# Feed-forward weights in runs of rows per partition, equal column groups, a block transposition on VectorE and a result kept by column groups

## The chip, the cores and the metric

The kernel runs on one core of a Trainium2 chip. The metric is the device time of one execution in microseconds; the median of three runs of the kernel before is 1333.5. Engines are named as the profile names them: PE is TensorE's matmul stream and PEld its weight loads, DVE is VectorE, ACT is ScalarE, POOL is GpSimd, SP is SyncE, which issues the large loads. All data are 32-bit floats.

## The reference, cut to what matters

One decoder block for one new token of each of two sequences (B = 2, D = 512, 32 heads of 128, 8192 cached positions, F = 1792):

```python
def _A_ref(x, k_cache, v_cache, wq, wo):
    q = (x @ wq).reshape(B, Sq, H, Dh).transpose(0, 2, 1, 3)
    scores = jnp.einsum("bhqd,bhkd->bhqk", q, k_cache) * (Dh ** -0.5)
    p = _softmax(scores, axis=-1)
    o = jnp.einsum("bhqk,bhkd->bhqd", p, v_cache)
    return o.transpose(0, 2, 1, 3).reshape(B, Sq, H * Dh) @ wo

def _B_ref(x, w_gate, w_up, w_down):
    return (_silu(x @ w_gate) * (x @ w_up)) @ w_down

h = x + _A_ref(_layernorm(x), k_cache, v_cache, wq, wo)
h2 = h + _B_ref(_layernorm(h), w_gate, w_up, w_down)
```

K and V together are 537 MB, the feed-forward weights 11 MB.

## The kernel before

**The stream.** Everything large goes through one ring of five slots of 4 MB, in the order in which it is used. `order` lists the transfers, `load` issues one on SP's queue, `pump` issues as many as slots are free, and `used` frees a slot. A K or V of one head of one sequence is one transfer, that of the last two pairs four pieces. The three feed-forward weights come last: `w_gate` and `w_up` in four pieces each (128 rows of the matrix, one on each partition, 7 KB a row), `w_down` in pieces of four, four, four, one and one blocks of 128 rows (2 KB a row). A DMA on SP also waits for the DMA eight before it, whose semaphore it takes over.

**Attention.** For pair i (a head and a sequence) VectorE multiplies K by q (L209) and sums (L212), the maximum goes over the partitions through PE (L224, L228, L230), ScalarE takes the exponential (L235), and PE multiplies P by V one pair later (`pv`, L250): 64 blocks of 128 x 128 with one-column weights, block j into column group j % 4 of the array, so that four matmuls run side by side. `project_o` (L273) adds the heads' part of the output into `attn`.

**The tail.** After the last pair come the residual `h1` (L330), the second norm (`layernorm`, L155 to L166) with four transpositions into `hT` (two of 32 columns used, the others zero), and then:

- `project_f` (L340), gate, then up: F is cut in 14 blocks of 128 columns that go round the four column groups, so two groups have four blocks (512 columns) and two have three (384). Each group's result lies on 32 partitions of the PSUM tile `psf`; two memsets (L305) fill what no matmul writes.
- `sg` is the gate times its sigmoid (L352, L353), `gu` the product with up (L356).
- Four transpositions on PE (L359) turn `gu`, and VectorE copies them to `gT` (L361).
- The down projection: 12 of the 14 blocks go round the column groups into `y_ps` (L371). VectorE and ScalarE copy it out in halves as `ysb` (L379, L380), and a matmul with `pick` (L385), a matrix of ones and zeros made at L310, sums the four groups into `f_ps`, which holds the residual already (L366) and to which the last two blocks add directly (L386).
- `res` is copied from `f_ps`, 2 x 512 (L390), and stored by SP (L391).

The schedule is manual: on every engine instructions run in the order of the code. A 32-bit matmul is two instructions of PE in the profile, each with a weight load.

Of the kernel before, what the change touches and what calls it, by code (L numbers as in the profile page):

```python
# [19 lines left out]
def tile_decode_block(  # L20
# [36 lines left out]
    # Everything large streams through one ring of equal slots, in the order of its use. A whole  # L57
    # K or V of one head is one transfer, but for the first and the last ones.
# [22 lines left out]
    order += [(("wg", 0), c, 1) for c in range(DC)] + [(("wu", 0), c, 1) for c in range(DC)]  # L81
    order += [(("wd", 0), c, n) for c, n in ((0, 4), (4, 4), (8, 4), (12, 1), (13, 1))]
# [5 lines left out]
    def load(item, e, n):  # L88
# [16 lines left out]
        elif kind == "wo":  # L105
            nc.sync.dma_start(
                t[:, : G * D].rearrange("p (c m) -> p c m", c=G),
                wo[i * G * DH : (i + 1) * G * DH, :].rearrange("(c p) m -> p c m", p=P),
            )
        elif kind in ("wg", "wu"):  # L110
            src = w_gate if kind == "wg" else w_up
            nc.sync.dma_start(t[:, e * F : (e + 1) * F], src[e * P : (e + 1) * P, :])
        else:
            nc.sync.dma_start(
                t[:, e * D : (e + n) * D].rearrange("p (c m) -> p c m", c=n),
                w_down[e * P : (e + n) * P, :].rearrange("(c p) m -> p c m", p=P),
            )
# [52 lines left out]
    xT_ps = layernorm(xs, "x")  # L170
# [129 lines left out]
    # Blocks of 128 columns go round the four column groups of the tensor engine.  # L300
    TAIL = FB % 4
    psf = []
    for n in range(2):
        t = psum.tile([P, 4, P], F32, name="wide", bufs=2)
        nc.vector.memset(t[64:, TAIL + 1 :, :], 0.0)  # L305
        psf.append(t)

    pick = const.tile([P, B], F32, name="pick")
    for b in range(B):
        nc.vector.tensor_reduce(  # L310
            pick[:, b : b + 1],
            ident.rearrange("p (t r) -> p r t", t=4)[:, b, :],
            axis=AX.X,
            op=OP.add,
        )

# [14 lines left out]
    hT_ps = layernorm(h1, "h")  # L331
    nc.vector.tensor_copy(hT[:, :, :B], hT_ps)

    def project_f(kind, ps):
        wt = slot[(kind, 0)]
        for c in range(DC):
            w = wt[:, c * F : (c + 1) * F].rearrange("p (k m) -> p k m", m=P)
            for t in range(4):
                nb = len(range(t, FB, 4))
                nc.tensor.matmul(  # L340
                    ps[32 * t : 32 * t + 32, :nb, :],
                    hT[:, c, :],
                    w[:, t::4, :],
# [20 lines left out]
    w = slot[("wd", 0)][:, : FB * D].rearrange("p (k m) -> p k m", k=FB)  # L364
    f_ps = psum.tile([B, D], F32, name="small", bufs=3)
    nc.tensor.matmul(f_ps, ident[:B, :B], h1, start=True, stop=False)  # L366
    y_ps = psum.tile([P, D], F32, name="wide", bufs=2)
    grouped = FB - TAIL
    for k in range(grouped):
        n, t = divmod(k, 4)  # L370
        nc.tensor.matmul(  # L371
            y_ps[32 * t : 32 * t + 32, :],
            gT[:, n, 32 * t : 32 * t + 32],
            w[:, k, :],
            start=(k < 4),
            stop=(k >= grouped - 4),
        )
    ysb = const.tile([P, D], F32, name="ysb")
    nc.vector.tensor_copy(ysb[:, : D // 2], y_ps[:, : D // 2])  # L379
    nc.scalar.activation(ysb[:, D // 2 :], y_ps[:, D // 2 :], AF.Copy)  # L380
    res = const.tile([B, D], F32, name="res")
    for k in range(grouped, FB):
        n, t = divmod(k, 4)
        if k == FB - 1:
            nc.tensor.matmul(f_ps, pick, ysb, start=False, stop=False)  # L385
        nc.tensor.matmul(  # L386
            f_ps, gT[:, n, 32 * t : 32 * t + B], w[:, k, :], start=False, stop=(k == FB - 1)
        )
    used(("wd", 0))
    nc.vector.tensor_copy(res, f_ps)  # L390
# [41 lines left out]
```

## Time and profile before

| | |
|---|---|
| three runs | 1332.21, 1333.50, 1333.54 us, median 1333.5 |
| the profiled execution, span of the core | 1329.8 us |
| DVE busy in the span | 1159.4 us (87%) |
| PE busy, weight loads | 585.3 us (44%), 374.0 us (28%) |
| ACT busy | 80.8 us (6%) |
| moved by DMA | 565.91 MB, mean 426 GB/s |

The span runs from the first to the last instruction of one profiled execution; the runs' times are those of whole executions and 2.4 to 3.7 us longer. Times in the rows are counted from the span's start. A timeline row gives the start, the length, the engine, the line, the operation, what it writes and reads, and in brackets how long the engine was idle before it and who ended that. [...] A DMA share is that of 16 DMA engines.

### The profile page before, as it was taken

Reading aid. Unit: us, or ns where it says so; the run is one execution under the profiler, and the core shown is the slowest. Engines: PE = TensorE matmul, PEld = TensorE weight load, DVE = VectorE, ACT = ScalarE, POOL = GpSimd, SP = SyncE. Lnnn points to the kernel's source line nnn. Section 1 sums busy time; section 2 is a strip of 40 time slices with the busy share of each in tenths; the row PEclk is TensorE's granted clock in tenths of the full one; section 3 lists DMA queues with packets and bytes.
Section 4 is the critical chain, followed back from the end, with each engine's and each line's share of the span. In section 5 each row is a group of like instructions: output and inputs, shape, how many; then the busy total and the mean of one; then the engine's idle time right before and its main releaser. Section 6 shows DMA issues by size and latency. Waiting matters only on the chain.

```text
span 1329.8 us, 19379 instructions
## 1 busy us (share of the span) xinstructions
PE 585.3 (44%) x9004; PEld 374.0 (28%) x9004; DVE 1159.4 (87%) x486; ACT 80.8 (6%) x341; POOL 1.9 (0%) x9
## 2 busy tenths in 40 slices
PE   5443433436633424433744334334375344344447
PEld 2322322223322322322412223222242222223322
DVE  6999999988899989997889989998879989999881
ACT  1000000000100000000100000000010000000001
POOL 0000000000000000000000000000000000000000
PEclk9656666667857566666886576666597666566668
DMA  9999999999999999999999999999999999999997
GB/s 398 437 432 433 430 433 430 435 429 428 432 432 432 433 430 434 431 429 435 427 430 436 428 438 427 436 428 429 431 414 433 431 433 431 434 430 433 422 401 279
DMA packets 30408, 565.91 MB, mean 426 GB/s; under 512 B 2676, under 2 KB 2676, under 8 KB 11640
## 3 DMA queue, kind: packets, MB, share of 16 engines
q1 hardware_dynamic: 30324, 564.67, 99.1%
q8 instruction: 70, 1.15, 0.3%
q14 instruction: 10, 0.08, 0.0%
q10 hardware_dynamic: 4, 0.00, 0.0%
HBM read 564.66 MB, written 0.00 MB: 425 GB/s over the span
## 4 chain that ended last, share of the span: by engine, by line
issue 98%; PE 1%; DVE 0%; DMA 0%; POOLq 0%; POOL 0%; ACT 0%
PE wide L340 1%; PE wide L371 0%; DMA xs<-in_A_x_dram 0%; PE small L385 0%; PE small L366 0%; PE small L386 0%; DVE gu L356 0%; DVE ln_stats L155 0%; DVE res L390 0%; PE small L359 0%; POOLq L427 0%; PE small L166 0%; DVE ln_y L163 0%; POOL ln_rstd L161 0%; DVE ysb L379 0%
## 5 line engine op out<-in xcount | busy, mean ns | idle before, releaser
L209 DVE TENSOR_TENSOR ring<-ring,qsb 128x4096 f32<-128x4096 f32 (+1 forms) x134 | 566.3, 4226 | 116.5 <-DMA ring<-in_A_k_cache_dram 105.5
L212 DVE TENSOR_REDUCE s<-ring 128x32 f32<-128x4096 f32 (+1 forms) x134 | 565.7, 4222 | 0.3
L250 PE MATMUL opart<-ring,p 128*1 128x128 f32 x8192 | 350.7, 351 | 165.2 <-DMA ring<-in_A_v_cache_dram 165.2
L250 PEld LDWEIGHTS opart<-ring,p 128*1 128x1 f32 x8192 | 247.1, 107 | 254.8 <-DMA ring<-in_A_v_cache_dram 170.2
L230 PE MATMUL small<-gm,nscale 1*128 1x1 f32 x128 | 35.8, 346 | 304.8 <-DVE gm L228 304.8
L224 PE MATMUL small<-ident,m 128*1 128x128 f32 x128 | 28.4, 310 | 210.3 <-DVE m L220 210.3
L230 PEld LDWEIGHTS small<-gm,nscale 1*128 1x128 f32 x128 | 30.3, 292 | 313.6 <-DVE gm L228 310.1
L224 PEld LDWEIGHTS small<-ident,m 128*1 128x1 f32 x128 | 5.5, 81 | 231.1 <-DVE m L220 228.8
L187 PE MATMUL wide<-ring,xb 128*128 128x512 f32 x128 | 58.7, 618 | 3.0 <-DMA ring<-in_A_wq_dram 3.0
L239 PE MATMUL small<-rs,ones 128*128 128x1 f32 x128 | 36.1, 351 | 46.9 <-ACT p L235 46.9
L263 ACT ACTIVATE osb<-opart 128x128 f32<-128x128 f32 x64 | 17.7, 277 | 530.6 <-PE opart L250 530.6
L239 PEld LDWEIGHTS small<-rs,ones 128*128 128x128 f32 x128 | 30.6, 297 | 52.4 <-ACT p L235 52.4
L273 PE MATMUL attn<-ring,oT 128*2 128x512 f32 x64 | 34.5, 698 | 0.3 <-ACT oT L266 0.3
L187 PEld LDWEIGHTS wide<-ring,xb 128*128 128x128 f32 x128 | 25.0, 198 | 34.1 <-issue 34.1
L232 ACT ACTIVATE nb<-small 128x1 f32<-128x1 f32 x64 | 10.9, 171 | 371.4 <-PE small L230 371.0
L265 PE MATMUL small<-r,osb 128*128 128x1 f32 x128 | 29.4, 299 | 2.0 <-ACT osb L263 2.0
L228 DVE TENSOR_REDUCE gm<-small 1x1 f32<-1x128 f32 x64 | 17.4, 272 | 14.7 <-PE small L224 14.7
L265 PEld LDWEIGHTS small<-r,osb 128*128 128x128 f32 x128 | 24.0, 235 | 20.6 <-issue 17.2
L266 ACT ACTIVATE oT<-small 128x1 f32<-128x1 f32 x64 | 11.0, 171 | 234.9 <-PE small L265 234.9
L235 ACT ACTIVATE p<-s,nb 128x64 f32<-128x64 f32 x64 | 22.3, 348 | 2.1
L243 DVE RECIPROCAL r<-small 128x1 f32<-128x1 f32 x64 | 10.1, 157 | 9.2 <-PE small L239 9.2
L220 DVE TENSOR_REDUCE m<-s 128x1 f32<-128x64 f32 x64 | 14.1, 220 | 2.2
(51 smaller groups left out, 66.1 us busy)
## 6 DMA issues: line engine op xcount, KB each, us to landing
ring<-in_A_k_cache_dram SPq DMA_DIRECT2D x61, 4096.0 KB, 39.8
ring<-in_A_v_cache_dram SPq DMA_DIRECT2D x61, 4096.0 KB, 30.8
ring<-in_A_k_cache_dram SPq DMA_DIRECT2D x12, 1024.0 KB, 19.6
ring<-in_A_v_cache_dram SPq DMA_DIRECT2D x12, 1024.0 KB, 19.8
ring<-in_A_wq_dram SPq DMA_DIRECT2D x4, 2048.0 KB, 35.2
ring<-in_A_wo_dram SPq DMA_DIRECT2D x4, 2048.0 KB, 17.2
ring<-in_B_w_gate_dram SPq DMA_DIRECT2D x4, 896.0 KB, 19.2
ring<-in_B_w_up_dram SPq DMA_DIRECT2D x4, 896.0 KB, 18.0
```

The source lines that it names most:

```text
L187: nc.tensor.matmul(ps, xb[:, c * B + b, :], w[:, c, n : n + 512], start=(c == 0), stop=(c == DC - 1),)
L209: nc.vector.tensor_tensor(kt, kt, qb, op=OP.mult)
L212: nc.vector.tensor_reduce(st[i]["s"][:, j0 : j0 + n], k_view(i, j0, n), axis=AX.X, op=OP.add)
L224: nc.tensor.matmul(st[i]["mrow"], st[i]["m"], ident, start=True, stop=True)
L228: nc.vector.tensor_reduce(gm, st[i]["mrow"], axis=AX.X, op=OP.max)
L230: nc.tensor.matmul(nb_ps, nscale, gm, start=True, stop=True)
L235: nc.scalar.activation(st[i]["p"], st[i]["s"], AF.Exp, bias=nb, scale=SCALE, accum_out=rs)
L239: nc.tensor.matmul(st[i]["den"], ones, rs, start=True, stop=True)
L250: nc.tensor.matmul(o[32 * t : 32 * t + 1, :], st[i]["p"][:, j : j + 1], vt[:, j, :], start=(j < 4), stop=(j >= NJ - 4),)
L263: nc.scalar.activation(osb, opart[i % 2], AF.Copy)
L265: nc.tensor.matmul(ot_ps, osb, st[i]["r"], start=True, stop=True)
L273: nc.tensor.matmul(attn, oT[:, h, :], w[:, h - g * G, :], start=(h == 0), stop=(h == H - 1))
```

## The change

- `order` and `load`: partition p of a slot now holds a run of neighbouring rows of the matrix, rows 4p to 4p+3 of `w_gate` and `w_up` and rows 14p to 14p+13 of `w_down`. `w_gate` is one transfer of 28 KB a partition, `w_up` two of 14 KB, `w_down` pieces of eight, four, one and one blocks (16, 8, 2 and 2 KB a partition).
- `layernorm` takes the columns for the second norm's transpositions in steps of four, to match.
- `project_f` gives each column group a quarter of F, 448 neighbouring columns. The memsets and `pick` are gone, and the two PSUM tiles are taken when they are used.
- `f_ps` becomes 128 x 128: column group t holds columns 128t to 128t+127 of the result on 32 partitions. Four matmuls put the residual there, ahead of the gate's.
- `gu` is written in the order (block, element), and one 32 x 32 block transposition on VectorE makes `gT` from it.
- The down projection adds all 14 blocks in all four column groups straight onto `f_ps`, 56 matmuls of 128 columns.
- `res` is 128 x 128; each sequence's row of the result leaves from four partitions, one by SP's queue and one by ScalarE's.

```diff
-    order += [(("wg", 0), c, 1) for c in range(DC)] + [(("wu", 0), c, 1) for c in range(DC)]
-    order += [(("wd", 0), c, n) for c, n in ((0, 4), (4, 4), (8, 4), (12, 1), (13, 1))]
+    order += [(("wg", 0), 0, DC)] + [(("wu", 0), c, 2) for c in range(0, DC, 2)]
+    order += [(("wd", 0), c, n) for c, n in ((0, 8), (8, 4), (12, 1), (13, 1))]
...
-            nc.sync.dma_start(t[:, e * F : (e + 1) * F], src[e * P : (e + 1) * P, :])
+            nc.sync.dma_start(
+                t[:, e * F : (e + n) * F],
+                src.rearrange("(p c) f -> p (c f)", p=P)[:, e * F : (e + n) * F],
+            )
         else:
             nc.sync.dma_start(
-                t[:, e * D : (e + n) * D].rearrange("p (c m) -> p c m", c=n),
-                w_down[e * P : (e + n) * P, :].rearrange("(c p) m -> p c m", p=P),
+                t[:, e * D : (e + n) * D],
+                w_down.rearrange("(p c) m -> p (c m)", p=P)[:, e * D : (e + n) * D],
             )
...
-            nc.tensor.transpose(yt[:, c, :], y[:, c * P : (c + 1) * P], ident[:B, :B])
+            cols = y.rearrange("b (p c) -> b c p", c=DC) if runs else y.rearrange("b (c p) -> b c p", c=DC)
+            nc.tensor.transpose(yt[:, c, :], cols[:, c, :], ident[:B, :B])
...
-    TAIL = FB % 4
-    psf = []
-    for n in range(2):
-        t = psum.tile([P, 4, P], F32, name="wide", bufs=2)
-        nc.vector.memset(t[64:, TAIL + 1 :, :], 0.0)
-        psf.append(t)
-
-    pick = const.tile([P, B], F32, name="pick")
-    for b in range(B):
-        nc.vector.tensor_reduce(
...
-    def project_f(kind, ps):
-        wt = slot[(kind, 0)]
+    f_ps = psum.tile([P, P], F32, name="small", bufs=3)
+    for t in range(4):
+        nc.tensor.matmul(
+            f_ps[32 * t : 32 * t + 32, :],
+            ident[:B, :32],
+            h1[:, t * P : (t + 1) * P],
+            start=True,
+            stop=False,
+        )
+
+    def project_f(kind):
+        ps = psum.tile([P, FQ], F32, name="wide", bufs=2)
         for c in range(DC):
-            w = wt[:, c * F : (c + 1) * F].rearrange("p (k m) -> p k m", m=P)
+            w = slot[(kind, 0)][:, c * F : (c + 1) * F]
             for t in range(4):
-                nb = len(range(t, FB, 4))
                 nc.tensor.matmul(
-                    ps[32 * t : 32 * t + 32, :nb, :],
+                    ps[32 * t : 32 * t + 32, :],
                     hT[:, c, :],
-                    w[:, t::4, :],
+                    w[:, t * FQ : (t + 1) * FQ],
...
-    gu = const.tile([P, 4 * P], F32, name="gu")
-    nc.vector.tensor_mul(gu, up, sg)
-    gT_ps = psum.tile([P, 4, P], F32, name="small", bufs=3)
-    for n in range(4):
-        nc.tensor.transpose(gT_ps[:, n, :], gu[:, n * P : (n + 1) * P], ident)
-    gT = const.tile([P, 4, P], F32, name="gT")
-    nc.vector.tensor_copy(gT, gT_ps)
...
+    gu = const.tile([P, FQ], F32, name="gu")
+    nc.vector.tensor_mul(
+        gu.rearrange("p (c j) -> p j c", c=FB),
+        up.rearrange("p (j c) -> p j c", c=FB),
+        sg.rearrange("p (j c) -> p j c", c=FB),
+    )
+    gT = const.tile([P, FQ], F32, name="gT")
+    nc.vector.transpose(gT, gu)
+
+    w = slot[("wd", 0)]
+    for c in range(FB):
+        for t in range(4):
+            nc.tensor.matmul(
+                f_ps[32 * t : 32 * t + 32, :],
+                gT[:, c * 32 : (c + 1) * 32],
+                w[:, c * D + t * P : c * D + (t + 1) * P],
+                start=False,
+                stop=(c == FB - 1),
+            )
     used(("wd", 0))
+    res = const.tile([P, P], F32, name="res")
     nc.vector.tensor_copy(res, f_ps)
-    nc.sync.dma_start(out.rearrange("b s d -> (b s) d"), res)
+    for b, queue in enumerate((nc.sync, nc.scalar)):
+        queue.dma_start(out[b, 0, :].rearrange("(t m) -> t m", t=4), res[b::32, :])
```

On SP's queue, the feed-forward weights at the end of the stream. Before (DMAHW names the semaphore of the transfer eight places earlier, DVE and PE the last user of the slot):

```order
L112 DMA ring<-in_B_w_gate_dram 128x1792 [waits DMAHW3_49,DVE_49]
L112 DMA ring<-in_B_w_gate_dram 128x1792 [waits DMAHW4_49]
L112 DMA ring<-in_B_w_gate_dram 128x1792 [waits DMAHW5_49]
L112 DMA ring<-in_B_w_gate_dram 128x1792 [waits DMAHW6_49]
L112 DMA ring<-in_B_w_up_dram 128x1792 [waits DMAHW7_49,DVE_49]
L112 DMA ring<-in_B_w_up_dram 128x1792 [waits DMAHW0_49]
L112 DMA ring<-in_B_w_up_dram 128x1792 [waits DMAHW1_49]
L112 DMA ring<-in_B_w_up_dram 128x1792 [waits DMAHW2_49]
L114 DMA ring<-in_B_w_down_dram 128x4x512 [waits DMAHW3_49,PE_49]
L114 DMA ring<-in_B_w_down_dram 128x4x512 [waits DMAHW4_49]
L114 DMA ring<-in_B_w_down_dram 128x4x512 [waits DMAHW5_49]
L114 DMA ring<-in_B_w_down_dram 128x512 [waits DMAHW6_49]
```

and now, with the store behind them:

```order
L112 DMA ring<-in_B_w_gate_dram 128x7168 [waits DMAHW3_49,DVE_49]
L112 DMA ring<-in_B_w_up_dram 128x3584 [waits DMAHW4_49,DVE_49]
L112 DMA ring<-in_B_w_up_dram 128x3584 [waits DMAHW5_49]
L117 DMA ring<-in_B_w_down_dram 128x4096 [waits DMAHW6_49,PE_49]
L117 DMA ring<-in_B_w_down_dram 128x2048 [waits DMAHW7_49]
L117 DMA ring<-in_B_w_down_dram 128x512 [waits DMAHW0_49]
L117 DMA ring<-in_B_w_down_dram 128x512 [waits DMAHW1_49]
L380 DMA out_dram<-res 4x128 [waits DMAHW3_49,DVE_49]
```

Thirteen transfers became seven. The first piece of `w_down` now waits for the transfer that held semaphore 6 (that of `wo`) instead of the first piece of `w_gate`.

On PE, from the last up matmuls on. Before:

```order
L359 MATMUL small<-ident,gu 128x128 [waits DVE_49]
L359 MATMUL small<-ident,gu 128x128 x3
L366 MATMUL small<-h_6392,ident 2x512
L371 MATMUL wide<-ring,gT 32x512 [waits DMAHW3_49,DVE_49]
L371 MATMUL wide<-ring,gT 32x512 x3
L371 MATMUL wide<-ring,gT 32x512 [waits DMAHW4_49]
L371 MATMUL wide<-ring,gT 32x512 x3
L371 MATMUL wide<-ring,gT 32x512 [waits DMAHW5_49]
L371 MATMUL wide<-ring,gT 32x512 x3
L386 MATMUL small<-ring,gT 2x512 [waits DMAHW6_49]
L385 MATMUL small<-ysb,pick 2x512 [waits Activation_49]
L386 MATMUL small<-ring,gT 2x512 [waits DMAHW7_49]
```

and now, from the second norm's last transpositions (L173) to the first 32 matmuls of the down projection (`small` is the pool name of `f_ps`):

```order
L173 MATMUL small<-ident,ln_y 128x2 x3
L327 MATMUL small<-h_6379,ident 32x128 x4
L340 MATMUL wide<-ring,hT 32x448 [waits DMAHW3_49,DVE_49,Pool_49]
L340 MATMUL wide<-ring,hT 32x448 x15
L340 MATMUL wide<-ring,hT 32x448 [waits DMAHW4_49]
L340 MATMUL wide<-ring,hT 32x448 x7
L340 MATMUL wide<-ring,hT 32x448 [waits DMAHW5_49]
L340 MATMUL wide<-ring,hT 32x448 x7
L369 MATMUL small<-ring,gT 32x128 [waits DMAHW6_49,DVE_49]
L369 MATMUL small<-ring,gT 32x128 x31
```

The residual's matmuls moved from behind `gu` to the place ahead of the gate's. Nothing stands between the last up matmul and the first down matmul now, and the down projection's only waits after its first are for its own weights.

## Rows read from the trace of the kernel before

**Rows 1.** The page: its first line, and the DMA line of the 40 slices.

```profile
span 1329.8 us, 19379 instructions
...
DMA  9999999999999999999999999999999999999997
```

**Rows 2.** Stages: length, busy us of PE, PEld, DVE, ACT, POOL, PEclk, DMA share, GB/s.

```profile
1200.00:1220.00 20.00, 8.35 (x136) 5.71 (x136) 18.53 (x8) 1.06 (x5) 0.00 (x0) 0.59 0.99 427
...
1270.00:1280.00 10.00, 6.68 (x96) 4.66 (x100) 9.97 (x8) 0.78 (x4) 0.00 (x0) 0.50 0.92 367
...
1300.00:1305.00 5.00, 4.34 (x132) 3.36 (x120) 0.02 (x1) 1.33 (x4) 0.00 (x0) 1.00 1.01 422
```

**Rows 3.** The timeline from the last P times V to the gate's first sets.

```profile
1299.75 3.67 PE L250 MATMUL opart<-ring,p 128*1 128x128 f32 x128
...
1308.54 0.58 PE L166 MATMUL small<-ident,ln_y 2*128 2x2 f32 x4 [3.06 <-DVE ln_y L163]
...
1309.42 1.07 PE L340 MATMUL wide<-ring,hT 128*32 128x512 f32 x4 [0.30 <-issue]
```

**Rows 4.** The timeline from the up matmuls to the store.

```profile
1314.81 0.13 PEld L340 LDWEIGHTS wide<-ring,hT 128*32 128x32 f32 x2 [0.27 <-issue]
...
1315.24 0.17 PEld L340 LDWEIGHTS wide<-ring,hT 128*32 128x32 f32 x6 [0.30 <-issue]
...
1318.93 0.69 DVE L356 TENSOR_TENSOR gu<-wide,sg 128x512 f32<-128x512 f32 x1 [2.11 <-PE wide L340]
...
1321.20 0.16 PEld L371 LDWEIGHTS wide<-ring,gT 128*32 128x32 f32 x8 [0.86 <-DVE gT L361]
...
1321.20 2.78 PE L371 MATMUL wide<-ring,gT 128*32 128x512 f32 x24
...
1324.05 0.42 DVE L379 COPY ysb<-wide 128x256 f32<-128x256 f32 x1 [3.00 <-PE wide L371]
...
1325.81 1.02 PE L386 MATMUL small<-ring,gT 128*2 128x512 f32 x2
...
1326.87 0.68 DVE L390 COPY res<-small 2x512 f32<-2x512 f32 x1 [2.39 <-PE small L386]
...
1327.57 0.33 SPq L391 DMA_DIRECT2D out_dram<-res  x1
```

**Rows 5.** Stages of one microsecond, columns as in rows 2.

```profile
1307.00:1308.00 1.00, 0.00 (x0) 0.00 (x0) 0.31 (x3) 0.00 (x0) 0.54 (x1) 0.70 1.07 431
...
1314.00:1315.00 1.00, 1.00 (x14) 0.29 (x8) 0.00 (x0) 0.00 (x0) 0.00 (x0) 0.88 1.01 377
...
1319.00:1320.00 1.00, 0.33 (x3) 0.33 (x4) 0.62 (x1) 0.00 (x0) 0.00 (x0) 1.00 0.53 205
...
1322.00:1323.00 1.00, 1.00 (x16) 0.31 (x12) 0.00 (x0) 0.00 (x0) 0.00 (x0) 1.00 0.25 96
```

**Rows 6.** The timeline: P times V of the pair before, at half clock.

```profile
1275.52 5.01 PE L250 MATMUL opart<-ring,p 128*1 128x128 f32 x96
```

**Rows 7.** The timeline: the maximum over partitions of the last pair.

```profile
1290.33 0.28 DVE L228 TENSOR_REDUCE gm<-small 1x1 f32<-1x128 f32 x1 [0.21 <-PE small L224]
```

**Rows 8.** Groups by shape from 1309 on: count, then busy us, mean ns of one.

```profile
L371 PEld LDWEIGHTS wide<-ring,gT 128*32 128x32 f32 x24 | 0.7, 109 | 2.1 <-issue 1.2 <-DVE gT L361 0.9
```

**Rows 9.** SP's timeline: the last piece of w_gate, the third of w_down.

```profile
1286.94 0.33 SPq L112 DMA_DIRECT2D ring<-in_B_w_gate_dram  x1
...
1303.21 7.71 SPq L114 DMA_DIRECT2D ring<-in_B_w_down_dram  x1
```

**Rows 10.** The tensor w_down: its five issues (ns, first and last start), and landing times.

```profile
L114 SPq DMA_DIRECT2D ring<-in_B_w_down_dram x5: 379/1604/7712, 1299.0 to 1313.7; - x5
...
DMA to landing us min/median/max: 9.6/18.0/18.8
```

**Rows 11.** DMA issues of 1286 to 1288: count, KB each, us to landing.

```profile
ring<-in_B_w_gate_dram SPq DMA_DIRECT2D x1, 896.0 KB, 18.9
```

**Rows 12.** The page, DMA queues: the instruction queue's packets, MB, share of 16 engines.

```profile
q8 instruction: 70, 1.15, 0.3%
```

More of the change, by code (lines that the diff above doesn't have):

```diff
@@ L149, in tile_decode_block, with layernorm @@
     oT = const.tile([P, H, B], F32, name="oT")
+    FQ = F // 4
     hT = const.tile([P, DC, 32], F32, name="hT")
     nc.gpsimd.memset(hT, 0.0)
-    def layernorm(src, tag):
+    def layernorm(src, runs):
         stats = work.tile([B, 6], F32, name="ln_stats")
@@ L165, in layernorm @@
         for c in range(DC):
-            nc.tensor.transpose(yt[:, c, :], y[:, c * P : (c + 1) * P], ident[:B, :B])
+            cols = y.rearrange("b (p c) -> b c p", c=DC) if runs else y.rearrange("b (c p) -> b c p", c=DC)
+            nc.tensor.transpose(yt[:, c, :], cols[:, c, :], ident[:B, :B])
         return yt
-    xT_ps = layernorm(xs, "x")
+    xT_ps = layernorm(xs, False)
     xT = const.tile([P, DC, B], F32, name="xT")
@@ L299, in tile_decode_block @@
                 project_o(i // B - G, i // B)
-    TAIL = FB % 4
-    psf = []
-    for n in range(2):
-        t = psum.tile([P, 4, P], F32, name="wide", bufs=2)
-        nc.vector.memset(t[64:, TAIL + 1 :, :], 0.0)
-        psf.append(t)
-    pick = const.tile([P, B], F32, name="pick")
-    for b in range(B):
-        nc.vector.tensor_reduce(
[L311 to L315, printed above, removed]
     i = NP - 1
@@ L330, in tile_decode_block @@
     nc.vector.tensor_add(h1, attn, xs)
[L331 removed]
+    hT_ps = layernorm(h1, True)
     nc.vector.tensor_copy(hT[:, :, :B], hT_ps)
[L334 to L335 removed]
+    f_ps = psum.tile([P, P], F32, name="small", bufs=3)
[9 more added lines that the diff above has]
+        ps = psum.tile([P, FQ], F32, name="wide", bufs=2)
         for c in range(DC):
[L337 removed]
+            w = slot[(kind, 0)][:, c * F : (c + 1) * F]
             for t in range(4):
[L339 removed]
                 nc.tensor.matmul(
[L341 removed]
+                    ps[32 * t : 32 * t + 32, :],
                     hT[:, c, :],
[L343 removed]
+                    w[:, t * FQ : (t + 1) * FQ],
                     start=(c == 0),
@@ L347, in project_f @@
         used((kind, 0))
-    gate, up = (t.rearrange("p k m -> p (k m)") for t in psf)
-    project_f("wg", psf[0])
-    sg = const.tile([P, 4 * P], F32, name="sg")
+        return ps
+    gate = project_f("wg")
+    sg = const.tile([P, FQ], F32, name="sg")
     nc.scalar.activation(sg, gate, AF.Sigmoid)
     nc.vector.tensor_mul(sg, gate, sg)
-    project_f("wu", psf[1])
-    gu = const.tile([P, 4 * P], F32, name="gu")
-    nc.vector.tensor_mul(gu, up, sg)
-    gT_ps = psum.tile([P, 4, P], F32, name="small", bufs=3)
@@ L358, in tile_decode_block @@
-    for n in range(4):
-        nc.tensor.transpose(gT_ps[:, n, :], gu[:, n * P : (n + 1) * P], ident)
-    gT = const.tile([P, 4, P], F32, name="gT")
-    nc.vector.tensor_copy(gT, gT_ps)
[L364 to L388, printed above, removed]
+    up = project_f("wu")
```

## The prediction

> **What bounds the kernel now.** The busy shares first: the DMA line is at nine tenths or more in 39 of 40 slices [rows 1], and late in the program the engines still move 427 GB/s at a share of 0.99 [rows 2]. So nearly all of the 1329.8 us is the streaming of K, V and weights, and the diff leaves that loop alone. What it can change is the tail, read from the timeline. The last head's attention starts at 1299.75, the second norm's four transpositions end at 1309.12, the gate matmuls start at 1309.42 [rows 3]. From there to the end one thing waits for the next: gate and up matmuls, product `gu`, transposition of `gu`, its copy, the down matmuls with the `ysb` detour, the copy to `res`, the store at 1327.57, the end at 1329.8 [rows 4]. That is 20.4 us, all on the path, and TensorE does most of it.
>
> [...] And the DMA engines are no longer all busy: their share is 0.53 at 1319 to 1320 and 0.25 at 1322 to 1323 [rows 5]. Some are through, the laggards are not, and a transfer has landed only when its slowest engine is done.
>
> **Gate and up.** 64 instructions in four column groups are 16 sets of four at once. Weight loads of successive sets start at 1314.81 and 1315.24, so a set of 512 columns takes 0.43 us at full clock [rows 4], twice that at half. [...] Two groups had 512 columns and two 384; the wide ones set the pace. With 448 in each, a set costs 0.376 us: 4.8 us at half are 6.4 sets, 9.6 more take 3.62 us, end 1317.86 + 0.2. Gain 0.84 us. The sigmoid and its product stay hidden: VectorE waited 2.11 us for the up matmuls before `gu` [rows 4].
>
> In front of the gate now stand the residual's matmuls into `f_ps`: four of 128 columns, 8 instructions. They wait for `h1` alone, so they fill the hole between 1309.12 and 1309.42 [rows 3], while VectorE copies `hT`. The price of such an instruction at a granted clock of 0.50 [rows 2] is 5.01 us / 96 = 52 ns [rows 6]: 0.42 us, of which 0.1 us sticks out, and that is worth 0.05 us once the clock has risen. Bounds 0 and 0.42. Before, this matmul ran under the copy of `gT` and cost nothing. The memsets and the sums for `pick` leave VectorE ahead of `gm`, which waited another 0.21 us for TensorE all the same [rows 7]: 0. The norm's transpositions now read every fourth column; I take 0, at most their 0.58 us again [rows 3].
>
> **Product and transposition.** A 512-column VectorE operation takes 0.69 us, a 256-column one 0.42 [rows 4], hence 1.05 ns per column and 0.15 fixed; 448 columns are 0.62 us. `gu` so gains 0.07; it now writes with a stride, and if that halved its rate it would lose 0.6. Gone are the four TensorE transpositions and the copy, 1319.62 to 1321.20 = 1.58 us [rows 4]. In their place comes one VectorE block transposition of 448 columns, which no row shows. Nearest is the copy: 0.62, with 0.09 for the two handovers. Bounds: 0.15 (the fixed part) and 1.24 (two passes for four-byte values). Gain 0.87 us. [...]
>
> **Down.** Before: 1321.20 to about 1326.83, with 24 grouped instructions, the copies of `ysb`, and six ungrouped 512-column ones [rows 4]: 5.63 us. Now: 14 blocks, four column groups of 128 columns, 112 instructions. The nearest row has the same moving shape and grouping: 128 instructions of P times V in 3.67 us at full clock [rows 3], 28.7 ns each, so 3.21 us, 3.25 with the 32-column loads. Gain 2.38. Those loads are the unknown: P times V loads one column. In before, eight 32-column loads take 0.16 us together while the matmuls run on [rows 4], which is within the 0.23 us of eight new instructions, so I take them as hidden. Lower bound: the row's own rate; upper bound under (b).
>
> **Result and store.** A copy of 128 columns on 128 partitions is 0.15 + 128 x 1.05 ns = 0.29 us against 0.68 [rows 4]: gain 0.39. Each half of the result leaves by its own queue; from issue to the end took 2.2 us [rows 4]; I add 0.1 for the second completion, bounds -0.3 and +0.33.
>
> **Sum.** -0.84 + 0.05 - 0.07 - 0.87 - 2.38 - 0.39 + 0.1 = -4.4 us. The profiled execution becomes 1325.4; it lies 3.7 us below the median of 1333.5, and I leave that as it is: **1329.1 us**.
>
> **What the weights allow.** On the new path the down matmuls start at about 1319.45 and need their last block at 1322.4. Before, issue plus landing gives: gate complete 1286.94 + 18.9 = 1305.8, third down piece 1303.21 + 18.8 = 1322.0, last one 1313.7 + 9.6 = 1323.3 [rows 9 to 11]. So the last piece, left as it is, would be late by 0.9 us. The change moves it: rows of 2 KB run at 205 / (0.53 x 16) = 24.2 GB/s per engine [rows 5], of 7 KB at 422 / (1.01 x 16) = 26.1, K and V at 427 / (0.99 x 16) = 27.0 [rows 2]. Each engine carries 229 KB of each weight. At 27.0, gate and up save 0.3 us each and the 12 of 14 blocks of down that lie in long rows 0.85: 1.4 us; I count 1.2. Last landing 1322.1, 0.3 us ahead of need; the first down piece has 6/14 of 229 KB behind it, 3.7 us, so it lands near 1318.4, ahead of 1319.45. Gate in one transfer need only be there by 1309.5, where 1305.8 is its whole: its cover is 3.7 us. Issue is no limit: SP stood 7.71 us in one down transfer of 2 KB rows [rows 9], which I take to have starved only the engines that were ahead, since the laggards had work queued; the new transfers make fewer, longer rows and are queued earlier.
>
> **Rivals.** (a) *The last weights set the end.* The long rows bring nothing, the last piece lands at 1323.3, eight matmuls and the run-out of 0.4 us follow, 1323.7 instead of 1322.7: gain 3.4, 1330.1. If an instruction fetch (16 KB, 0.3% x 16 x 1329.8 us / 70 = 0.91 us [rows 12]) falls on a lagging engine too, 1331.0. For: the margin is 0.3 us. Against: the rates above.
>
> (b) *The loads of the down matmuls are not hidden.* A load that can start only when its group's matmul has ended adds its own 109 ns [rows 8] to each of 28 sets: +3.1, 1332.2, no change that can be measured. Against: eight loads in 0.16 us while matmuls run [rows 4]. [...]
>
> (c) *The clock falls in the new hole.* TensorE rests from 1318.05 to 1319.45, 1.4 us, where before it rested only while `gu` was made, 0.7 [rows 4]. Down at half clock is 112 x 52 ns [rows 6] = 5.85 us, +2.6: 1331.7. Against: before the fall (0.70 in 1307 to 1308, at no matmul at all [rows 5]) it had been idle for most of the 5 us between the end of P times V, 1303.42, and the norm's transpositions at 1308.54 [rows 3]; 1.4 us between two busy stretches is far less.
>
> (d) *Slower: the long rows run badly.* If rows of 28 and 16 KB went at the instruction fetch's pace, 16.4 KB in 0.91 us = 18.0 GB/s [rows 12], 688 KB per engine would take 38.2 us instead of about 27: last landing 1334, end some 7.5 us after before's, 1341. It decides once the last landing is past 1326.9, 4.4 us after need. Against: K and V rows of 32 KB are the fastest of all.
>
> **How the numbers follow.** The sum 0.62; (a) 0.17; (b) 0.10; (c) 0.08; (d) 0.03. A measurement of this kernel can tell about 0.2%, 2.7 us, from no change: faster means under 1330.8. That holds for the sum but for 0.02 (transposition and stride both at their worst), and for 0.10 of (a): 0.70. Within 0.2%: 0.02, the rest of (a), (b), 0.07 of (c): 0.26. Slower: (d) and 0.01 of (c) with worse beside it, 0.04. Range: down to 1328.0 (transposition at its bound, stores at theirs, and the 1.3 us by which the runs differ), up to 1331.8, which takes in (a) and (c) and leaves (b) and (d), 0.13, and the odd tail outside.
>
> **What would show it.** Right: up matmuls end about 0.8 us earlier after the gate's start; the block transposition near 0.6 us; 112 down instructions within 3.3 us at clock 1.00 without a hole; the result's copy at 0.29; span near 1325.4. (a) shows as a hole among the last down matmuls released by a DMA of w_down, (b) as an even spacing near 0.22 us per set, (c) as a granted clock under 1.00 after 1319, (d) as gate matmuls waiting for w_gate. Wrong altogether: a store that takes over 1 us longer, or a transposition of 2 us or more.

## The result, and the profile after

The changed kernel takes 1337.8 us (median of five runs, 1337.4 to 1338.2), beside 1332.4 for the kernel before on the same chip (five runs, 1331.7 to 1333.5). The ratio is 1.0041, 95% interval 1.0030 to 1.0052: slower by 5.4 us, where 1329.1 had been forecast and nothing above 1331.8 was in its range. The profiled execution spans 1336.0 us against 1329.8 [rows 1].

The page of the kernel after: its first line, the DMA line of the slices, and VectorE's multiplication of K by q (busy us, mean ns, and after the second bar the idle time before it and its releaser):

```profile
span 1336.0 us, 19536 instructions
...
DMA  9999999999999999999999999999999999999997
...
L216 DVE TENSOR_TENSOR ring<-ring,qsb 128x4096 f32<-128x4096 f32 (+1 forms) x134 | 566.3, 4226 | 124.3 <-DMA ring<-in_A_k_cache_dram 111.0
```

The DMA engines are as full as before [rows 1], and VectorE's own work has not changed by a tenth of a microsecond, but it stands idle ahead of this multiplication for 124.3 us, 111.0 of them ended by the DMA of K. The same row of before:

```profile
L209 DVE TENSOR_TENSOR ring<-ring,qsb 128x4096 f32<-128x4096 f32 (+1 forms) x134 | 566.3, 4226 | 116.5 <-DMA ring<-in_A_k_cache_dram 105.5
```

So VectorE is idle 7.8 us more, and 5.5 of them end with the DMA of K: not in the feed-forward part that was rewritten, but in the stream of K and V, whose code has not changed. Where it is lost is read from the timeline of VectorE, at the same instructions of both kernels. Before:

```profile
527.48 4.43 DVE L209 TENSOR_TENSOR ring<-ring,qsb 128x4096 f32<-128x4096 f32 x1 [1.40 <-DMA ring<-in_A_k_cache_dram]
...
1192.92 4.42 DVE L209 TENSOR_TENSOR ring<-ring,qsb 128x4096 f32<-128x4096 f32 x1 [1.25 <-DMA ring<-in_A_k_cache_dram]
```

and after:

```profile
530.80 4.43 DVE L216 TENSOR_TENSOR ring<-ring,qsb 128x4096 f32<-128x4096 f32 x1 [1.53 <-DMA ring<-in_A_k_cache_dram]
...
1200.17 4.43 DVE L216 TENSOR_TENSOR ring<-ring,qsb 128x4096 f32<-128x4096 f32 x1 [1.48 <-DMA ring<-in_A_k_cache_dram]
```

3.3 us late at 530, 7.3 at 1200: it grows with the time, about 6 ns in every microsecond. There is no one event to look for; the loads take about 0.6% longer throughout. Stages of 100 us show it directly (columns as in rows 2, GB/s last). Before, and then after:

```profile
400.00:500.00 100.00, 39.44 (x712) 27.72 (x716) 91.51 (x36) 5.30 (x25) 0.00 (x0) 0.64 1.00 432
...
900.00:1000.00 100.00, 50.56 (x696) 30.70 (x686) 80.76 (x33) 6.97 (x26) 0.00 (x0) 0.70 1.00 425
```

```profile
400.00:500.00 100.00, 38.02 (x680) 26.76 (x680) 91.11 (x36) 5.30 (x25) 0.00 (x0) 0.64 1.00 429
...
900.00:1000.00 100.00, 48.63 (x706) 31.09 (x706) 81.47 (x32) 7.09 (x27) 0.00 (x0) 0.69 1.00 419
```

A share of 1.00 in all four, and 429 for 432, 419 for 425 GB/s: the engines don't wait, they are slower. The trace's records of the single packets, of which a transfer is made, give the size: the 15616 packets of 32 KB took 1215.9 ns each on average before and 1220.9 after. At 976 of them per DMA engine that is 5.0 us more; over packets of every length it is 6.7.

The tail, from the second norm's transpositions to the store, is the part that was forecast. Its timeline after:

```profile
1316.05 0.63 PE L173 MATMUL small<-ident,ln_y 2*128 2x2 f32 x4 [3.06 <-DVE ln_y L169]
...
1317.19 8.36 PE L340 MATMUL wide<-ring,hT 128*32 128x448 f32 x64
...
1325.62 0.91 DVE L358 TENSOR_TENSOR gu<-wide,sg 128x448 f32<-128x448 f32 x1 [1.81 <-PE wide L340]
1326.57 0.65 DVE L364 STREAM_TRANSPOSE gT<-gu 128x448 f32<-128x448 f32 x1
...
1327.64 4.93 PE L369 MATMUL small<-ring,gT 128*32 128x128 f32 x112 [2.10 <-DMA ring<-in_B_w_down_dram]
1332.63 0.29 DVE L378 COPY res<-small 128x128 f32<-128x128 f32 x1 [5.42 <-PE small L369]
1332.95 0.65 SPq L380 DMA_DIRECT2D out_dram<-res  x1
```

The transpositions start at 1316.05 instead of 1308.54 [rows 3]: 7.5 us of lateness are there before the first changed matmul. From there to the end it takes 19.95 us instead of 21.26, a gain of 1.3 and not 4.4. 7.5 - 1.3 = 6.2 us is the whole difference of the spans. Two questions follow: what slows the stream, and what became of 3.1 us in the tail.

### The profile page after: what moved, and what is told of

The parts are those of the page before. It is cut to its first block, busy times and chain, and to the rows that moved or that the text cites. A ratio compares the mean times of both kernels' runs of the same rounds, so it can differ in the third digit from the quotient of the medians.

```text
span 1336.0 us, 19536 instructions
## 1 busy us (share of the span) xinstructions
PE 581.1 (43%) x9088; PEld 375.7 (28%) x9088; DVE 1158.4 (87%) x481; ACT 80.4 (6%) x340; POOL 1.9 (0%) x9
## 4 chain that ended last, share of the span: by engine, by line
DMA 62%; DVE 33%; PE 5%; issue 0%; ACT 0%; SPq 0%; DVEq 0%
DMA ring<-in_A_k_cache_dram 51%; DVE s L219 16%; DVE ring L216 16%; DMA ring<-in_A_v_cache_dram 8%; DMA ring<-in_B_w_down_dram 2%; PE wide L194 2%; PE opart L257 1%; PE attn L280 1%; DMA ring<-in_A_wq_dram 1%; DVE m L227 0%; PE small L369 0%; PE small L231 0%; DVE r L250 0%; DVE gm L235 0%; ACT qsb L201 0%
## 5 line engine op out<-in xcount | busy, mean ns | idle before, releaser
L216 DVE TENSOR_TENSOR ring<-ring,qsb 128x4096 f32<-128x4096 f32 (+1 forms) x134 | 566.3, 4226 | 124.3 <-DMA ring<-in_A_k_cache_dram 111.0
L231 PE MATMUL small<-ident,m 128*1 128x128 f32 x128 | 28.2, 307 | 207.1 <-DVE m L227 207.1
```

Source lines behind the costliest of these rows:

```text
L216: nc.vector.tensor_tensor(kt, kt, qb, op=OP.mult)
L231: nc.tensor.matmul(st[i]["mrow"], st[i]["m"], ident, start=True, stop=True)
```

## What slows the stream

The change leaves `order`'s K and V alone, but not the memory. The constants lie ahead of the ring in each partition. `pick`, `ysb` and a `res` of 2 KB are gone, `sg`, `gu` and `gT` are 1792 bytes instead of 2048, and the ring's first slot starts at byte 32992 of each partition, where it started at 37376. 37376 is 146 x 256; 32992 lies 224 above a multiple of 256. Theory: the start of the slots costs the half per cent. Rivals: something in the changed instructions or the smaller memory does, or the forecast's (d), the longer rows of the weights.

**The ring put back on a multiple of 256, in the kernel after.** An unused tile of 32 bytes moves its start to 33024 = 129 x 256:

```diff
+    const.tile([P, 8], F32, name="pad")
```

> The changed kernel with an unused tile of 32 bytes per partition at the end of the constants, so that the ring's slots start at byte 33024 of each partition (a multiple of 64) instead of 32992 (32 over a multiple of 64). No instruction differs. Address theory: the stream's lateness of 7.8 us at the gate's start goes away, 32 KB packets go back to the length they have in the kernel before, and what is left is the tail: about 1329 us. Program theory (longer program, long rows, second queue): nothing changes, 1337.8 us.

Measured: 1329.0 us (10 runs, 1328.5 to 1329.5) beside 1331.9, ratio 0.9975 (0.9966 to 0.9984). The same two VectorE instructions:

```profile
527.41 4.42 DVE L216 TENSOR_TENSOR ring<-ring,qsb 128x4096 f32<-128x4096 f32 x1 [1.40 <-DMA ring<-in_A_k_cache_dram]
...
1193.03 4.43 DVE L216 TENSOR_TENSOR ring<-ring,qsb 128x4096 f32<-128x4096 f32 x1 [1.51 <-DMA ring<-in_A_k_cache_dram]
```

They are within about 0.1 us of before's. The packets of 32 KB are back at 1215.9 ns. 32 bytes that nobody reads or writes are worth 8.7 us: 6.8 of them by the gate's start (1310.42 for 1317.19), most of the rest in the tail, as told below. With 1329.3 us (8 runs, ratio 0.9976, 0.9965 to 0.9986) a second set of runs, beside the version with both changes at once below, gave the same:

> The kernel after with an unused tile of 32 bytes more (ring at byte 33024 of each partition) once more, beside the two others on the same chip: 1328.5 to 1329.5 us, ratio 0.9975. It is the measure for the version above: a difference under 0.7 us between the two can't be told from none.

**The ring moved off it, in the kernel before.** The same edit, with tiles of 32, 64, 128 and 256 bytes, so that nothing differs but the addresses of the ring and of the small working tiles behind it:

```diff
+    const.tile([P, 8], F32, name="pad")
```

> The kernel before with the same unused tile of 32 bytes, so that the ring starts at byte 37408 instead of 37376, 32 over a multiple of 64. No instruction differs. Address theory: slower by about 7.8 us, 1340 us, with the lateness growing evenly through the stream. Program theory: no change, 1332.4 us.

> The kernel before with an unused tile of 64 bytes: ring at byte 37440, a multiple of 64 and not of 128. If a multiple of 64 is enough: 1332.4 us. If 128 or more is needed: between that and 1340 us.

> The kernel before with an unused tile of 128 bytes: ring at byte 37504, a multiple of 128 and not of 256. The ring at multiples of 512 (before) and of 256 (the changed kernel with 32 bytes) has 32 KB packets of 1213 ns, at 64 and at 32 over a multiple of 64 it costs 6.9 and 8.1 us. If 128 is enough: 1332 us. If 256 is needed: about 1339 us.

> The kernel before with an unused tile of 256 bytes more in the const pool: the ring's slots start at byte 37632 of each partition (a multiple of 256, not of 512) instead of 37376. If what counts is that the start is a multiple of 256, as the kernel after with 32 bytes more was (33024), this is the kernel before again: ratio 1.000, 1331 to 1334 us, the last attention's DVE sum of K and the gate's start within 1 us of before's (1309.4). If any move of the ring, or any byte more in the const pool, costs what 32, 64 and 128 bytes cost (6.9 to 8.1 us), or if 512 is the step, it takes 1338 to 1341 us, ratio 1.005 to 1.006.

And one where 32 bytes are added behind the ring, in the work pool, so that the working tiles move and the ring stays:

```diff
+    work.tile([P, 8], F32, name="pad", bufs=1)
```

> The kernel before with the ring left at byte 37376 and only the small working tiles behind it (q, scores, P, statistics) moved by 32 bytes. If the address of the transfers' destination is what counts: no change, 1332.4 us. If it is the engines' operands beside the ring: slower, up to 1340 us.

| kernel before with | ring starts at | above a multiple of 256 | median, us | ratio (95%) |
|---|---|---|---|---|
| nothing | 37376 | 0 | 1331.9 to 1332.5 | 1 |
| 32 bytes ahead | 37408 | 32 | 1340.0 | 1.0057 (1.0042 to 1.0072) |
| 64 bytes ahead | 37440 | 64 | 1338.8 | 1.0050 (1.0035 to 1.0065) |
| 128 bytes ahead | 37504 | 128 | 1339.3 | 1.0054 (1.0037 to 1.0070) |
| 256 bytes ahead | 37632 | 0 | 1332.1 | 0.9997 (0.9988 to 1.0006) |
| 32 bytes behind | 37376 | 0 | 1332.5 | 1.0004 (0.9994 to 1.0013) |

The trace of the first of them has the marks of the kernel after. The page's row of VectorE's multiplication, and the gate's start:

```profile
L209 DVE TENSOR_TENSOR ring<-ring,qsb 128x4096 f32<-128x4096 f32 (+1 forms) x134 | 566.3, 4226 | 123.1 <-DMA ring<-in_A_k_cache_dram 110.4
```

```profile
1317.64 2.79 PE L340 MATMUL wide<-ring,hT 128*32 128x512 f32 x14 [0.31 <-issue]
```

123.1 us idle and a gate at 1317.64, 8.2 us after before's 1309.42 [rows 3], with not one instruction changed. The packets are the same as before's in number and length, and each takes longer: those of 32 KB 1220.8 ns for 1215.9, of 8 KB 317.6 for 312.0, of 7 KB 277.4 for 272.5, of 2 KB 89.5 for 87.3. That is 2 to 6 ns a packet from 2 to 32 KB, a price by the packet more than by the byte, and over all packets 8.0 us per engine of the 8.2 by which the gate is late. With 256 bytes ahead (32 KB packets of 1216.0 ns) the gate is back:

```profile
1309.40 9.45 PE L340 MATMUL wide<-ring,hT 128*32 128x512 f32 x64 [0.31 <-issue]
```

So the start of the slots is shown to be the cause, and a multiple of 256 bytes to be enough. Offsets of 32, 64 and 128 cost about the same in the kernel before, 6.9 to 8.1 us or 0.5 to 0.6%, and 224 costs 6.8 us of the stream in the kernel after; other offsets were not run. That a move as such costs nothing, nor a byte more in memory, is shown by the last two rows.

In shares, with 32 bytes ahead the packets of 32 KB took 0.4% longer and those of 8 KB 1.8%. An offset of 224 cost no more than one of 32: the packets of 32 KB took 1220.9 ns at 224 (the kernel after) and 1220.8 at 32. What in a packet takes the time no run here shows.

## What became of the tail

With the ring back in place, the first experiment shows the tail without that disturbance. Its timeline:

```profile
1309.28 0.64 PE L173 MATMUL small<-ident,ln_y 2*128 2x2 f32 x4 [3.06 <-DVE ln_y L169]
...
1309.84 0.65 PE L327 MATMUL small<-h,ident 2*32 2x128 f32 x8
...
1310.42 8.91 PE L340 MATMUL wide<-ring,hT 128*32 128x448 f32 x64
...
1319.41 0.91 DVE L358 TENSOR_TENSOR gu<-wide,sg 128x448 f32<-128x448 f32 x1 [1.81 <-PE wide L340]
1320.36 0.65 DVE L364 STREAM_TRANSPOSE gT<-gu 128x448 f32<-128x448 f32 x1
...
1321.05 3.00 PEld L369 LDWEIGHTS small<-ring,gT 128*32 128x32 f32 x112 [2.53 <-DVE gT L364]
1321.06 3.26 PE L369 MATMUL small<-ring,gT 128*32 128x128 f32 x112 [1.73 <-DVE gT L364]
1324.39 0.29 DVE L379 COPY res<-small 128x128 f32<-128x128 f32 x1 [3.39 <-PE small L369]
1324.71 0.65 SPq L381 DMA_DIRECT2D out_dram<-res  x1
```

Each stage runs from one row's start to the next, the last to the span's end, so the columns add up (before from rows 3 and 4, "forecast" is before with the forecast's terms):

| stage, us | before | forecast | after | after, ring at 33024 |
|---|---|---|---|---|
| transpositions to gate | 0.88 | 0.93 | 1.14 | 1.14 |
| gate to `gu` | 9.51 | 8.67 | 8.43 | 8.99 |
| `gu` to down | 2.27 | 1.33 | 2.02 | 1.65 |
| down to `res` | 5.67 | 3.29 | 4.99 | 3.33 |
| `res` to store | 0.70 | 0.31 | 0.32 | 0.32 |
| store to the end | 2.23 | 2.33 | 3.05 | 2.99 |
| sum | 21.26 | 16.86 | 19.95 | 18.42 |

With the ring in place the tail gains 2.8 us of the forecast's 4.4, and three terms were too good: `gu`, the residual's matmuls, the store. In the kernel after, two more things happen in the down projection. Its first matmul waits for its weights, and then TensorE's clock is down (stages, columns as in rows 2; PEclk, third from the end, is the granted TensorE clock as a share of its full speed; the second block is a stage of the same matmuls with the ring in place):

```profile
1328.00:1329.00 1.00, 1.00 (x36) 1.00 (x31) 0.00 (x0) 0.00 (x0) 0.00 (x0) 0.69 0.48 195
1328.50:1331.50 3.00, 3.00 (x65) 3.00 (x59) 0.00 (x0) 0.00 (x0) 0.00 (x0) 0.50 0.30 111
```

```profile
1322.00:1323.00 1.00, 1.00 (x48) 1.00 (x40) 0.00 (x0) 0.00 (x0) 0.00 (x0) 1.00 0.12 47
```

The granted clock, 0.69 in 1328 to 1329 and 0.50 from 1328.5 to 1331.5, fell within the first microsecond of the matmuls and stayed down for most of the stage, which took 1.7 us longer (4.99 for 3.33). This is the forecast's rival (c). Ahead of it TensorE had rested 2.10 us; with the ring in place it rested 1.73, and the granted clock stayed at 1.00. The longer rest is a wait for `w_down`. The tensor w_down in the kernel after, and with the ring in place:

```profile
L117 SPq DMA_DIRECT2D ring<-in_B_w_down_dram x4: 328/355/422, 1298.0 to 1303.0; - x4
...
DMA to landing us min/median/max: 28.3/29.5/31.6
```

```profile
L117 SPq DMA_DIRECT2D ring<-in_B_w_down_dram x4: 328/355/422, 1290.2 to 1294.7; - x4
...
DMA to landing us min/median/max: 28.2/29.1/31.1
```

The first piece, of eight blocks, lands 29.5 us after 1298.0, at 1327.5, 10.3 us after the gate's start; with the ring in place at 1290.2 + 29.1 = 1319.3, 8.9 after. It was issued 7.8 us later, where the gate's start was only 6.8 later, and took 0.4 us longer to land. Beside it gate and up were through 0.56 us sooner in the kernel after (8.43 for 8.99 in the table), so the need came earlier too. Together they made the first down matmul late by 0.4 us (2.02 for 1.65 in the table). What of this is the slower packets' doing, and why the clock fell, no run separates.

**`gu` and the residual's matmuls.** Three kernels took up the missed terms, all with the ring on a multiple of 256. In the first, `gu` is written as it comes and up and `sg` are read in steps, and the residual's matmuls stand behind the up matmuls (the lines that move them, and the tile of 32 bytes, are left out here):

```diff
-    nc.vector.tensor_mul(
-        gu.rearrange("p (c j) -> p j c", c=FB),
-        up.rearrange("p (j c) -> p j c", c=FB),
-        sg.rearrange("p (j c) -> p j c", c=FB),
-    )
+    nc.vector.tensor_mul(
+        gu.rearrange("p (c j) -> p c j", c=FB),
+        up.rearrange("p (j c) -> p c j", c=FB),
+        sg.rearrange("p (j c) -> p c j", c=FB),
+    )
```

> The changed kernel with the ring at a multiple of 256 (as e1_after_pad32, 1329.0 us), gu written in order and its two operands read with a stride instead, and the residual's four matmuls behind the up matmuls, in TensorE's hole. If the strided write is what made gu 0.91 us: 0.62 us, and strided reads cost nothing; if any stride does, 0.91 again. The gate's start should come 0.2 us after the end of the norm's transpositions less than now. Together 0.4 to 0.5 us: 1328.5 us.

1329.5 us, ratio 0.9980 (0.9971 to 0.9989): not to be told from the 0.9975 without the edit. Its timeline:

```profile
1309.36 8.58 PE L331 MATMUL wide<-ring,hT 128*32 128x448 f32 x64 [0.31 <-issue]
...
1318.00 0.91 DVE L357 TENSOR_TENSOR gu<-wide,sg 128x448 f32<-128x448 f32 x1 [1.81 <-PE wide L331]
...
1319.64 3.73 PE L368 MATMUL small<-ring,gT 128*32 128x128 f32 x112 [1.36 <-DVE gT L363]
1321.71 1.03 PEld L368 LDWEIGHTS small<-ring,gT 128*32 128x32 f32 x40 [0.38 <-DMA ring<-in_B_w_down_dram]
1322.94 0.16 PEld L368 LDWEIGHTS small<-ring,gT 128*32 128x32 f32 x8 [0.20 <-DMA ring<-in_B_w_down_dram]
```

The gate starts 0.31 us after the transpositions again, `gu` still takes 0.91 (steps cost as much on the reading side), and the down matmuls, which now start earlier, stop twice for a DMA of w_down and end hardly sooner: `res` begins 15.0 us after the norm's transpositions (1308.41 in this run), where it was 15.1. So the residual's matmuls kept the gate back by 0.2 us (0.95 from the transpositions to the gate here, 1.14 with them ahead of it), and behind them stands rival (a): the last weights, which here let go of TensorE at 1322.94, take back whatever else is saved ahead of them.

**The store.** Both halves on SP's queue, to tell the second queue from the shape:

```diff
-    for b, queue in enumerate((nc.sync, nc.scalar)):
+    for b, queue in enumerate((nc.sync, nc.sync)):
```

> As e1_after_pad32, but both halves of the result leave by SP's queue. From issue to the end it now takes 3.0 us against 2.2 in the kernel before, and each issue 0.65 against 0.33 us. If two queues issuing at once are the cause: 0.33 us each, one after the other, and an end about 0.3 to 0.6 us earlier, 1328.5 us. If the shape (four rows of 512 bytes) is the cause: 0.65 us each, one after the other, 1329.4 us.

1329.6 us, 0.9982 (0.9973 to 0.9992), and the two issues stand one behind the other:

```profile
1324.96 1.22 SPq L381 DMA_DIRECT2D out_dram<-res  x2
```

0.61 us each, where the store of 2 x 512 took 0.33 [rows 4]: dear without a second queue. From issue to the end it is 3.3 us, with two queues 3.0.

**Both at once.** In the last version TensorE reads the gate's and up's weights in steps of 14 columns, so that `sg` and `gu` are contiguous on both sides, and the result is copied onto two partitions, so that each queue stores 1 KB from two neighbouring ones. The residual's matmuls stand behind up, and the ring starts at 34816 = 136 x 256:

```diff
-                    ps[32 * t : 32 * t + 32, :],
+                    ps[32 * t : 32 * t + 32, :].rearrange("p (c j) -> p c j", c=FB),
                     hT[:, c, :],
-                    w[:, t * FQ : (t + 1) * FQ],
+                    w[:, t * FQ : (t + 1) * FQ].rearrange("p (j c) -> p c j", c=FB),
...
+    for n, (queue, copy) in enumerate(((nc.sync, nc.vector.tensor_copy), (nc.scalar, nc.scalar.copy))):
+        res = const.tile([B, 2, P], F32, name=f"res{n}")
+        for t in range(2):
+            k = 2 * n + t
+            copy(res[:, t, :], f_ps[32 * k : 32 * k + B, :])
+        queue.dma_start(out[:, 0, 2 * n * P : 2 * (n + 1) * P].rearrange("b (t m) -> b t m", t=2), res)
```

> The kernel after with the ring back on a multiple of 256, the residual's matmuls behind the up matmuls, and two more changes: TensorE reads the gate's and up's weights with a stride of 14 columns, so that sg and gu are contiguous on both sides; and the result is copied out of f_ps by four copies of 2 x 128 (two on DVE, two on ACT) onto two partitions, so that each queue stores rows of 1 KB from two neighbouring partitions. If a stride in the VectorE operation is what made gu take 0.91 us, gu takes 0.62; the down matmuls then start about 0.3 us earlier but their last weights land at 1322.9 all the same, and the down matmuls end near 1323.4. If the shape of four rows on partitions 32 apart is what made the store dear, its issue falls from 0.65 to about 0.33 us and from issue to the end it takes 2.2 us again instead of 3.0. Together 0.7 to 1.0 us less than the kernel after with 32 bytes more: span near 1326.5, 1328.0 to 1328.6 us, ratio 0.997. If TensorE is slowed by reading weights at a stride of 56 bytes, the gate and up matmuls take over 9.5 us instead of 8.9, and the gain is gone: 1329 to 1333 us; if a store's cost is that of a second queue, issue stays at 0.6 us.

1332.1 us, 0.9997 (0.9989 to 1.0006): no gain at all is left. Its timeline, and two stages of its gate and up matmuls:

```profile
1309.55 12.48 PE L331 MATMUL wide<-ring,hT 128*32 128x448 f32 x64 [0.31 <-issue]
...
1311.06 0.20 PEld L331 LDWEIGHTS wide<-ring,hT 128*32 128x32 f32 x4 [0.57 <-issue]
1311.84 0.20 PEld L331 LDWEIGHTS wide<-ring,hT 128*32 128x32 f32 x4 [0.58 <-issue]
...
1317.19 0.18 PEld L331 LDWEIGHTS wide<-ring,hT 128*32 128x32 f32 x4 [0.58 <-issue]
...
1317.96 0.19 PEld L331 LDWEIGHTS wide<-ring,hT 128*32 128x32 f32 x4 [0.58 <-issue]
...
1322.09 0.62 DVE L357 TENSOR_TENSOR gu<-wide,sg 128x448 f32<-128x448 f32 x1 [4.94 <-PE wide L331]
...
1327.39 0.32 SPq L378 DMA_DIRECT2D out_dram<-res  x1
1327.45 0.53 ACT L377 COPY res<-small 2x128 f32<-2x128 f32 x2 [10.95 <-DVE res L377]
1328.01 0.25 ACTq L378 DMA_DIRECT2D out_dram<-res  x1
```

```profile
1309.00:1312.00 3.00, 2.69 (x18) 0.94 (x22) 0.17 (x1) 0.00 (x0) 0.00 (x0) 0.50 1.00 425
...
1318.00:1321.00 3.00, 3.00 (x20) 0.72 (x16) 0.00 (x0) 0.00 (x0) 0.00 (x0) 1.00 0.46 192
```

Two sets at full clock with contiguous weights, in the first experiment:

```profile
1316.53 0.12 PEld L340 LDWEIGHTS wide<-ring,hT 128*32 128x32 f32 x4 [0.26 <-issue]
1316.90 0.12 PEld L340 LDWEIGHTS wide<-ring,hT 128*32 128x32 f32 x4 [0.26 <-issue]
```

The matmuls take 12.48 us instead of 8.9, though the clock is granted in full (1.00) from 1315 on: a set of four starts every 0.77 us (1317.19, 1317.96), with contiguous weights every 0.37 (1316.53, 1316.90), as forecast. At half clock (0.50) the steps cost next to nothing: the sets start 0.78 us apart (1311.06, 1311.84), the contiguous ones of the first experiment 0.75. So the steps took from TensorE what the higher clock gives. The two suspicions that this version was made for are borne out all the same: without steps `gu` takes 0.62 us, just the forecast's figure, and with two rows of 1 KB from neighbouring partitions an issue takes 0.25 to 0.32 us and the end comes 2.2 us after the last (1330.2 - 1328.01), as in before [rows 4]. It is the shape, four rows of 512 bytes from partitions 32 apart, that makes a store dear; whether the count, the length or the distance does was not separated. The copies cost that gain: ScalarE's began only when VectorE's were through.

The steps here are 56 bytes in the weights and up to 128 in `gu`, and both engines were slower with them: VectorE took 0.91 us for 0.62, and TensorE at full clock 0.77 us a set for 0.37, at half clock 0.78 for 0.75. Why a step costs this no run here shows.

**Fine pieces.** The long rows in before's thirteen transfers instead of seven, again with the ring at 33024:

```diff
-    order += [(("wg", 0), 0, DC)] + [(("wu", 0), c, 2) for c in range(0, DC, 2)]
-    order += [(("wd", 0), c, n) for c, n in ((0, 8), (8, 4), (12, 1), (13, 1))]
+    order += [(("wg", 0), c, 1) for c in range(DC)] + [(("wu", 0), c, 1) for c in range(DC)]
+    order += [(("wd", 0), c, n) for c, n in ((0, 4), (4, 4), (8, 4), (12, 1), (13, 1))]
```

> As e1_after_pad32, with the feed-forward weights in the transfers of the kernel before (13 of them; rows of 7, 7 and 8 and 2 KB) at the new places. If long rows and few transfers bring the last landing forward by the 0.8 us seen between the two kernels: the last landing 0.4 to 0.8 us later after the last piece of V, still ahead of the down matmuls' end, so 1329.0 to 1329.6 us. If they bring nothing: no difference in the landing.

1329.0 us, 0.9975 (0.9965 to 0.9984): the same as with seven. The last piece landed at 1308.1 + 15.0 = 1323.1, 12.4 us after the gate's start, with seven 12.5. Rows of 7 and 8 KB in thirteen transfers do as well as rows of 28, 14 and 16 KB in seven: that cut is worth nothing that can be measured here.

## Why the prediction was wrong, point by point

- **The step that failed** is in its first paragraph: "nearly all of the 1329.8 us is the streaming of K, V and weights, and the diff leaves that loop alone". The first half was right, and should have been the warning; the second half took the code of the loop for the loop. The diff drops or shortens six tiles that lie ahead of the ring, and 0.6% of 1310 us weighs more than all that was forecast for the tail. In its place the runs showed that the loop's packets take longer once the ring starts off a multiple of 256, 7.5 us by the norm's transpositions, and that 32 unused bytes take this away. No rival had it: (d) looked for slow rows in the weights alone, and 1341 lies on the right side by chance.
- **Gate and up** (-0.84): -0.52 with the ring in place, -1.08 in the kernel after. The set of 448 columns is as forecast, 0.37 us at full clock and 0.75 at half; the difference is when the clock rises, 4.4 to 5.5 us after the gate's start, for which the forecast took 4.8. In before it rose at about 1314.24, 4.8 us after the gate's start at 1309.42 [rows 3]: the granted clock was 0.50 in 1313 to 1314, 0.88 in 1314 to 1315 [rows 5] and 1.00 in 1315 to 1316. The forecast's 0.2 us of run-out no row shows by itself; with it the forecast had 8.67 us from the gate to `gu`, and 8.99 and 8.43 were measured.
- **The residual's matmuls** (+0.05): +0.2. They took 0.65 us, not 0.42, so more of them stuck out; within the bounds. The norm's transpositions in steps of four, taken at 0, took 0.64 us for 0.58.
- **`gu`** (-0.07): +0.22. The forecast named the stride and its price of up to 0.6, and then took none.
- **The transposition** (0.62 us): 0.65. Right. The two passes behind its upper bound of 1.24 were a supposition that no run shows.
- **Down** (3.25 us): 3.26, with the ring in place. Right: 29 ns per instruction, and the 32-column loads hidden. Rival (b) falls: 112 loads of all rows, 3.00 us together, ran within the 3.26 of as many matmuls. In the kernel after the stage took 4.99 us by rival (c), which had 0.08 and a rest of 1.4 us where 2.10 were measured.
- **Result** (-0.39): -0.38. Right.
- **The store** (+0.1, bounds -0.3 and +0.33): +0.8, outside its bounds. The forecast priced the second queue; what cost was the new shape of the source, which it didn't price.
- **The weights**: with the ring in place the last piece was issued at 1294.7 and landed 28.2 us later, at 1322.9; the forecast had 1322.1, before's time was 1323.3. As the forecast took it, the slowest part sets that time: the sixteen landings of before's last piece run from 1317.6 to 1323.3. The margin of 0.3 us was not there. That it didn't show is because the clock, `gu` and the residual made the need later; where the residual was moved and the clock rose sooner, rival (a) held.

The sum is -4.4 forecast, -2.8 measured, once the ring is on a multiple of 256. That the padded kernel's 1329.0 us is the forecast's 1329.1 is therefore partly luck: the before of these runs has a median of 1331.9, 1.6 us below the one that the forecast started from. Nor was the step of 3.7 us from span to time a fixed one: in the runs here a whole execution took 1.7 to 1.9 us longer than its own span, so the profiled execution of before was one of about 1331.6, below the median. Span against span, 1325.4 was forecast, and 1336.0 and with the padding 1327.7 measured.

## What to carry to other kernels

Ahead of pricing an edit, ask what lies behind the tiles whose size it changes: a buffer that is streamed into for the whole run should keep its start on a multiple of 256 bytes (every other start tried here cost 0.5 to 0.6%), and an unused tile that keeps it there pays. A small loss that grows evenly with the time points to the rate of everything, not to a place; compare the same instruction at three times of the run before looking at any one stage. And price an access pattern by itself: each pattern with steps here (the product, 0.91 us for 0.62; the moving weights at full clock, 0.77 for 0.37; the store's four partitions, 0.65 for 0.33) took longer than the contiguous one beside it.

## What the runs showed of the hardware

- The address in a partition to which a DMA writes mattered: 0.5 to 0.6% of the stream for starts of 32, 64, 128 and 224 bytes above a multiple of 256, nothing that can be measured for 0 (four starts). Off the multiple a packet of 2 to 32 KB took 2 to 6 ns longer.
- A 32-bit VectorE product of 448 columns takes 0.62 us contiguous and 0.91 with steps, whether the written or the read side has them; TensorE reading its moving values at steps of 56 bytes needs 0.77 us for a set of four column groups of 448, twice the contiguous 0.37 at full clock and as good as the contiguous 0.75 at half clock.
- A store of 2 KB took 0.61 to 0.65 us to issue and 3.0 from issue to the end with a source of four rows of 512 bytes on partitions 32 apart, 0.25 to 0.32 and 2.2 with two rows of 1 KB on neighbouring ones.
- 112 weight loads of 32 columns over all rows, going round the column groups, ran beside as many matmuls: 3.00 us of loads within 3.26.
- After 2.10 us of rest TensorE's granted clock fell to 0.50 in the down matmuls (one profile); after 1.73 it stayed at 1.00 (two profiles with the ring in place; in two more, after 1.72, the stage took the same 3.26 and 3.27 us). What decides it stays open.
